# Attention's elementwise steps moved from GpSimd to VectorE and ScalarE, with longer scans and products

## The chip, the cores and the metric

The kernel runs on one core of a Trainium2 chip. Its time is the device time of one execution, in microseconds, as the median of the runs shown. The profile is of one execution on that core. PE is TensorE, DVE is VectorE, ACT is ScalarE, POOL is GpSimd and SP is the engine that issues most DMAs. [...]

## The reference, cut to what matters

An attention with complex decays, then two mixing stages. B=4 batches, H=8 heads, S=768 tokens, D=48.

```python
scale = np.minimum(mag, 0.999) / (mag + 1e-06)      # mag = |a_re + i a_im|
a_re_n, a_im_n = (a_re * scale, a_im * scale)
for t in range(S):
    new_re = ar * S_re - ai * S_im                  # ar, ai: a_re_n, a_im_n of token t
    new_im = ar * S_im + ai * S_re
    S_re, S_im = (new_re + k v^T, new_im)
    y[:, :, t] = q . S_re
...
h = x^T @ U @ V;  u = x + h^T                       # first stage, tokens mixed with rank 32
x = u + np.maximum(u @ w_ch1, 0.0) @ w_ch2          # width 384, hidden 1536
...
u = x + real(fft2(x));  un = layer norm of u        # second stage
out = u + np.maximum(un @ w_ch1, 0.0) @ w_ch2
```

## The kernel before, in words

The attention is worked in 24 chunks of 128 tokens (6 per batch), and its elementwise part in 12 pairs of chunks (PAIRS), 3 per batch. A tile of a pair is 128 partitions by 768 elements: 3 groups of channels, 2 chunks, 128 tokens.

`decays(m)` makes, for pair m, the running products of the decays and from them the scaled queries and keys. Its steps stand in order: squares of the parts of a (ACT), a range count (line 291, DVE), logarithm and exponential (line 87, ACT), `1 - 2e-6 s` (line 325, POOL, or DVE for the first batch), a product with a minimum (line 326, DVE), the tangent (line 337, POOL), a running product as three scans of 256 elements (line 340, DVE), a Newton step of the inverse root (lines 349, 353 and 354, two on POOL and one on DVE), and the two products with q and k (lines 359 and 360). `turns(m)` turns these tangents into angles (line 87, ACT), sums them along the tokens as three more scans (line 381, DVE), reduces them to one turn (lines 389 and 390), takes sine and cosine (ACT) and multiplies: per chunk four products of 384 elements (lines 408 and 409), three on DVE and one on POOL. The result QK goes through six DMAs per chunk into QT (line 412, SP).

`products(m, j)` does the matrix products of one chunk: scores (line 437), their mask (line 442, DVE), transposes of the keys (line 451), outputs y and state g (line 469). From the fifth chunk of batch 1 on the products are made of float16 parts: a cast on ACT (lines 445, 460, 486, 500, 567) and the remainder (lines 446 and 568 on POOL; 461, 487 and 501 on DVE). The keys are scaled once more in place (line 494, POOL).

The first mixing stage runs over b, g (halves of 384 tokens) and f (12 slices of the hidden width). For each f, `mm3` (lines 91 to 93) makes hp = w1 u from (hi, lo) pairs in three products; ACT makes hh = relu(hp) (line 182), DVE its remainder hl (line 184), and a step later lines 91 to 93 add w2 hh, w2 hh and w2 hl into acc. The attention of batch b+1 runs beside the first stage of batch b: `Side` hands out its steps. `make_ut` transposes x (line 617), copies it to SBUF (line 622, ACT), adds the low-rank token part from another PSUM bank (lines 626 and 627) and splits the sum into a pair u (lines 629 and 630). `from_f64` and `load_w` (lines 108 to 142) make float32 pairs of the float64 weights. The DFT and the second mixing stage follow.

The framework's scheduler sets the order on each engine from a simulated timeline and from priorities that the code gives (hh and hl are high), and each engine runs its instructions strictly in that order.

Of the kernel before, what the change touches and what calls it, by code (L numbers as in the profile page):

```python
# [13 lines left out]
I16 = mybir.dt.int16  # L14
AF = mybir.ActivationFunctionType
# [6 lines left out]
DM = H * D  # L22
# [19 lines left out]
def mixer_kernel(ctx, tc, a_in, qk_in, v_in, u_in, v4_in, w_in, cc_in, ss_in, cb_in, sb_in, id_in, mask_in, rows_in, out):  # L42
# [69 lines left out]
    def from_f64(src, name, signs=False):  # L112
# [22 lines left out]
    def load_w(mi, f, z):  # L135
# [4 lines left out]
        x = from_f64(w_in[mi, f][:, zs], f"w{mi}_{f}_{z}", mi == 1 or f > 8)  # L140
# [50 lines left out]
    # ------------------------------------------------------------------ attention  # L191
# [40 lines left out]
    def load_vs():  # L232
        """All values of the first batch."""
# [18 lines left out]

    def parts(m):
        """The first pair goes chunk by chunk, so that its products start early."""
        return [slice(0, 1), slice(1, 2)] if m == 0 else [slice(0, 2)]

    def decays(m):
        """Decayed queries and keys of a pair of chunks and the tangents of its turns."""
# [3 lines left out]
        E = G if b else V  # L262

# [3 lines left out]
        if b == 0:  # L267
            T_, s1, s2 = a[:, 1], mk("L"), mk("s")
            qf, kf = qk[:, 0], qk[:, 1]
        else:  # L270
            T_, s1, s2 = mk("T"), mk("L"), mk("s")
            qf, kf = s1, s2
        Th = a[:, 0] if b == 0 else mk("Th")
# [3 lines left out]
        ew[m] = T_, Th, qf, kf, ends  # L277
# [26 lines left out]
        for js in jj:  # L304
            re, im, s1_, s2_ = of(js, a[:, 0], a[:, 1], s1, s2)
            if at_once:
# [5 lines left out]
                steady(js)  # L312
# [22 lines left out]
        for js in jj:  # L335
# [3 lines left out]
            for i in range(3):  # L339
                V.tensor_tensor_scan(out=row(s1, i, js), data0=starts[:, :n], data1=row(s1, i, js), initial=1.0, op0=ALU.max, op1=ALU.mult)  # L340
# [3 lines left out]
        for js in jj:  # L344
            s1_, s2_, th = of(js, s1, s2, Th)
            tabled(s2_, s1_, AF.Ln)
            tabled(s2_, s2_, AF.Exp, bias=lnhalf, scale=-0.5, accum_out=stat("decay", b, cc[js.start]))
            A.activation(th, s2_, AF.Square, scale=2.0)
            (G if m == 2 or b else V).tensor_tensor(th, s1_, th, ALU.mult)
        yield  # L350
        for js in jj:
            s1_, s2_, th = of(js, s1, s2, Th)
            V.scalar_tensor_tensor(out=s2_, in0=th, scalar=3.0, in1=s2_, op0=ALU.subtract, op1=ALU.mult, reverse0=True)
            (G if m in (1, 2) or b else V).tensor_tensor(s1_, s1_, s2_, ALU.mult)
            V.tensor_copy(ends[:, :, js], s1_[:, :, :, 127])
# [869 lines left out]
```

## Time and profile before

| | |
|---|---|
| median of 3 runs | 1040.34 us (1038.24 to 1041.38) |
| span of the profiled execution, first to last instruction | 1035.1 us |
| its own time | not recorded beside the span; the median lies 5.2 us above the span |
| busy: PE, DVE, ACT, POOL | 885.1, 690.3, 441.3, 443.3 us |
| mean granted TensorE clock | 0.949 |

The span has five parts. Until 78 us the first batch's elementwise work runs and PE is mostly idle. Until 130 us the first batch's products run. From 130 to 518 us the first mixing stage runs with the attention of the later batches beside it. From 518 to 725 us that stage ends, and the weights of the second are made. From 725 us the second stage runs alone.

A busy engine is not always working: the duration of an instruction in the trace holds the time for which it could not go on.

### The profile page before, as it was taken

The page shows a single profiled execution, that of the slowest core. Times are in us where ns is not written, and L with a number is a line of the kernel's source. Part 1 is how long each engine was busy: PE and PEld are TensorE (multiplying, and loading weights), DVE is VectorE, ACT ScalarE, POOL GpSimd, SP SyncE. Part 2 cuts the span into 40 slices and gives each one's busy share as a digit, 9 for nine tenths or more (in the row PEclk, how much of TensorE's full clock was granted, in tenths as well). Part 3 has the DMA queues.
Part 4 walks back from the last instruction along what each step waited for, and adds up shares of the span by engine and source line. Part 5 has one row for each costly group of instructions (what it writes and reads, how often), then busy time and mean ns, then how long its engine had stood idle before and what let it go on. Part 6 is the DMA issues. An engine that isn't in the chain of part 4 may idle for free. (4 is left out here: it accounts for less than half of the span.)

```text
span 1035.1 us, 16471 instructions
## 1 busy us (share of the span) xinstructions
PE 885.1 (86%) x6338; PEld 841.7 (81%) x6338; DVE 690.3 (67%) x1104; ACT 441.3 (43%) x841; POOL 443.3 (43%) x426
## 2 busy tenths in 40 slices
PE   0059978788778787798899999779999999999997
PEld 0048777578777787787899999779999999999997
DVE  7997988897877689788764727886535554362121
ACT  6436565657545555555643224465212211222111
POOL 4445646575464645656446307776312222020000
PEclk9999899979898898989899999889999999999999
DMA  8078646834516152614135103342101021000000
GB/s 346 0 103 165 194 81 138 166 69 109 94 45 121 49 93 69 115 48 93 33 61 200 39 1 115 108 144 77 62 16 47 2 77 46 1 23 19 7 23 27
DMA packets 47097, 83.43 MB, mean 81 GB/s; under 512 B 5600, under 2 KB 36064, under 8 KB 47008
## 3 DMA queue, kind: packets, MB, share of 16 engines
q1 hardware_dynamic: 45152, 75.96, 30.8%
q0 software_dynamic: 1856, 6.31, 1.7%
q8 instruction: 52, 0.85, 0.4%
q14 instruction: 37, 0.30, 0.1%
HBM read 53.79 MB, written 9.44 MB: 61 GB/s over the span
## 5 line engine op out<-in xcount | busy, mean ns | idle before, releaser
L184 DVE SCALAR_TENSOR_TENSOR hl<-hp,hh 128x384 fp32r<-128x384 f32 x192 | 105.4, 551 | 191.8 <-ACT hh L182 186.6
L182 ACT ACTIVATE hh<-hp 128x384 fp32r<-128x384 f32 x192 | 93.1, 488 | 270.9 <-PE hp L93 249.1
L91 PE MATMUL acc<-w,hh 128*128 128x384 f32 x576 | 202.4, 352 | 2.0 <-ACT hh L182 2.0
L93 PE MATMUL acc<-w,hl 128*128 128x384 f32 x576 | 166.1, 352 | 38.4 <-DVE hl L184 38.2
L92 PE MATMUL acc<-w,hh 128*128 128x384 f32 x576 | 197.4, 343 | 0.0
L93 PEld LDWEIGHTS acc<-w,hl 128*128 128x128 f32 x576 | 106.9, 195 | 45.4 <-DVE hl L184 45.1
L91 PEld LDWEIGHTS acc<-w,hh 128*128 128x128 f32 x576 | 111.4, 193 | 4.3 <-ACT hh L182 3.0
L92 PEld LDWEIGHTS acc<-w,hh 128*128 128x128 f32 x576 | 111.5, 194 | 0.0
L91 PE MATMUL hp<-u,w 128*128 128x384 f32 x288 | 103.0, 359 | 6.2 <-ACT w L141 3.1
L92 PE MATMUL hp<-u,w 128*128 128x384 f32 x288 | 103.7, 360 | 1.2 <-POOL u L630 1.0
L93 PE MATMUL hp<-u,w 128*128 128x384 f32 x288 | 102.4, 356 | 0.0
L92 PE MATMUL hp<-n,w 128*128 128x384 f32 x288 | 96.9, 336 | 1.6 <-DVE n L920 1.6
L91 PE MATMUL hp<-n,w 128*128 128x384 f32 x288 | 96.5, 336 | 1.1 <-ACT n L919 1.1
L93 PE MATMUL hp<-n,w 128*128 128x384 f32 x288 | 96.8, 336 | 0.0
L437 PE MATMUL sc<-QT 96*128 96x128 f32 x384 | 66.6, 328 | 11.4 <-DMA QT<-QK 10.5
L437 PEld LDWEIGHTS sc<-QT 96*128 96x128 f32 x384 | 60.7, 232 | 14.3 <-issue 11.3
L142 POOL TENSOR_TENSOR w<-wxw,w 128x384 fp32r<-128x384 f32 x48 | 58.8, 1235 | 21.9 <-ACT w L141 21.7
L451 PE MATMUL kp<-ident,QK 128*128 128x128 f32 x120 | 20.5, 297 | 53.7 <-POOL QK L409 48.6
L91 PEld LDWEIGHTS hp<-u,w 128*128 128x128 f32 x288 | 58.5, 203 | 7.0 <-ACT w L141 3.3
L451 PEld LDWEIGHTS kp<-ident,QK 128*128 128x128 f32 x120 | 16.1, 155 | 55.5 <-POOL QK L409 48.6
L92 PEld LDWEIGHTS hp<-u,w 128*128 128x128 f32 x288 | 58.6, 203 | 2.2 <-POOL u L630 1.6
L93 PEld LDWEIGHTS hp<-u,w 128*128 128x128 f32 x288 | 58.3, 203 | 0.0
(302 smaller groups left out, 2056.4 us busy)
## 6 DMA issues: line engine op xcount, KB each, us to landing
QT<-QK SPq DMA_DIRECT2D x144, 129.0 KB
stw<-in_w_dram SPq DMA_DIRECT2D x48, 384.0 KB
ain<-in_a_dram SPq DMA_DIRECT2D x12, 768.0 KB
qkin<-in_qk_dram SPq DMA_DIRECT2D x12, 768.0 KB
x1d<-x SPq DMA_DIRECT2D x24, 192.0 KB
vin<-in_v_dram SPq DMA_DIRECT2D x18, 192.0 KB
lo<-x1d SPq DMA_DIRECT2D x12, 192.0 KB
out_dram<-lo SPq DMA_DIRECT2D x12, 192.0 KB
```

The lines of the kernel that those rows point to most:

```text
L91: T.matmul(o, ah, bh, start=start, stop=False, skip_group_check=skip)
L92: T.matmul(o, ah, bl, start=False, stop=False, skip_group_check=skip)
L93: T.matmul(o, al, bh, start=False, stop=stop, skip_group_check=skip)
L142: G.tensor_tensor(w[:, 1, zs], x, f32(w[:, 0, zs]), ALU.subtract)
L182: A.activation(hh, hp, AF.Relu)
L184: V.scalar_tensor_tensor(out=hl, in0=hp, scalar=0.0, in1=f32(hh), op0=ALU.max, op1=ALU.subtract)
L437: T.matmul(ps[:, h, :], q[:, 128:256], q[:, :128], start=True, stop=True)
L451: T.transpose(kp[z][:, i * 128 : (i + 1) * 128], QK[:, z, i, 128:256], ident)
```

## The change

- Moved from POOL to DVE: lines 349, 354, 446, 556, 568 and 630, part of 359 and 551, and the sign of the weights (line 128, which becomes the DVE form of line 130 everywhere).
- Moved from POOL or DVE to ACT: lines 325, 389 (later batches) and 494. The count of line 291 becomes two Relu passes with a sum on ACT for the later batches.
- Merged: three scans of 256 elements become one of 768, with a reset in a uint8 tile; the four products of a chunk's turn become two of 768, all on DVE, with sine and cosine in one tile `turn` of one buffer.
- `make_ut`: the low-rank product is added into the bank of the transposes, so that the copy of line 622 and the sum of line 627 go for all but the first group; u is split from PSUM.
- Buffers: tag t from 6 to 4, `turn` 1 of twice the size, vl from 2 to 1.

```diff
-            (V if z else G).tensor_tensor(QK[:, z, :, 128:256], kf[:, :, j], w[:, :, j], ALU.mult)
+                w = turn[:, :, :, j]
+                for to, x in ((slice(128, 256), kf), (slice(0, 128), qf)):
+                    V.tensor_tensor(QK[:, :, :, to], x[:, :, j].unsqueeze(1).to_broadcast([128, 2, 3, 128]), w, ALU.mult)
...
-            for i in range(3):
-                V.tensor_tensor_scan(out=row(s1, i, js), data0=starts[:, :n], data1=row(s1, i, js), initial=1.0, op0=ALU.max, op1=ALU.mult)
+            V.tensor_tensor_scan(out=flat(s1), data0=starts, data1=flat(s1), initial=1.0, op0=ALU.max, op1=ALU.mult)
...
+                if cy is not None:
+                    V.tensor_tensor(T_[:, :, 0, 0], T_[:, :, 0, 0], cy[:, :3], ALU.add)
+                V.tensor_tensor_scan(out=flat(Th), data0=going, data1=flat(T_), initial=0.0, op0=ALU.mult, op1=ALU.add)
...
-            (G if m == 2 or b else V).tensor_tensor(th, s1_, th, ALU.mult)
+            V.scalar_tensor_tensor(out=th, in0=s1_, scalar=FSCALE**2, in1=th, op0=ALU.mult, op1=ALU.mult)
...
-            E.tensor_scalar(s2_, s2_, -2e-6, 1.0, ALU.mult, ALU.add)
+            A.activation(s2_, s2_, AF.Copy, bias=1.0, scale=-2e-6)
...
+                    A.activation(Th[:, :, js], re, AF.Relu, bias=least, scale=-1.0, accum_out=stat("im", b, cc[0]))
+                    A.activation(Th[:, :, js], s2_, AF.Relu, bias=most, accum_out=stat("im", b, cc[1]))
...
-                for z in range(2):
-                    G.tensor_tensor(QK[:, z, :, 128:256], QK[:, z, :, 128:256], QK[:, z, :, 256:257].to_broadcast([128, 3, 128]), ALU.mult)
+                for i in range(3):
+                    A.activation(QK[:, :, i, 128:256], QK[:, :, i, 128:256], AF.Copy, scale=QK[:, 0, i, 256:257])
...
-                G.tensor_tensor(plo[:, hs], pm[hf], ph[:, hs], ALU.subtract)
+                V.tensor_tensor(plo[:, hs], pm[hf], ph[:, hs], ALU.subtract)
...
-            G.tensor_tensor(slo, sS, shi, ALU.subtract)
+            V.tensor_tensor(slo, sS, shi, ALU.subtract)
...
+            zv = bank(f"zv{b}_{g}_{k}")[:, :384] if first else xs[k]
+            T.matmul(zv, zst[b][:, k * 128 : (k + 1) * 128], vst[:, g * 384 : (g + 1) * 384], start=first, stop=True, skip_group_check=not first)
```

The first place is VectorE in the first mixing stage, batch 1, at the turn of pair (2, chunks 2 and 3): QK is the turned result, hl the remainder that PE waits for, kl and vl remainders of float16 parts, pm the masked scores. Before:

```order
L408 TENSOR_TENSOR QK2_2_2909<-L2_2_2630,Th2_2_2632 128x3x128
L487 SCALAR_TENSOR_TENSOR vl2_2_3102<-vin2_2_2932,vh2_2_3101 128x384
L184 SCALAR_TENSOR_TENSOR hl0_1_0_2_2806<-hp0_1_0_2_2734,hh0_1_0_2_2804 128x384
L442 TENSOR_TENSOR pm2_1_1_2895<-sc2_1_1_2863,mask_82 128x512
L461 SCALAR_TENSOR_TENSOR kl2_1_2900<-kp2_1_0_2903,kh2_1_2899 128x8x48
L405 COPY QK2_3_2934<-fe2_2_2634 128x6x2
L408 TENSOR_TENSOR QK2_3_2934<-L2_2_2630,T2_2_2629 128x3x128
L409 TENSOR_TENSOR QK2_3_2934<-s2_2_2631,T2_2_2629 128x3x128
L408 TENSOR_TENSOR QK2_3_2934<-L2_2_2630,Th2_2_2632 128x3x128
L461 SCALAR_TENSOR_TENSOR kl2_1_2900<-kp2_1_1_2926,kh2_1_2899 128x8x48
L184 SCALAR_TENSOR_TENSOR hl0_1_0_3_2861<-hp0_1_0_3_2824,hh0_1_0_3_2859 128x384
```

Now:

```order
L181 SCALAR_TENSOR_TENSOR hl0_1_0_3_2787<-hp0_1_0_3_2750,hh0_1_0_3_2785 128x384
L419 COPY QK2_3_2858<-fe2_2_2561 128x6x2
L423 TENSOR_TENSOR QK2_2_2835<-s2_2_2559,turn2_2_2557 128x6x128
L423 TENSOR_TENSOR QK2_2_2835<-L2_2_2558,turn2_2_2557 128x6x128
L423 TENSOR_TENSOR QK2_3_2858<-s2_2_2559,turn2_2_2557 128x6x128
L423 TENSOR_TENSOR QK2_3_2858<-L2_2_2558,turn2_2_2557 128x6x128
L476 SCALAR_TENSOR_TENSOR kl2_1_2826<-kp2_1_0_2829,kh2_1_2825 128x8x48
L476 SCALAR_TENSOR_TENSOR kl2_1_2826<-kp2_1_1_2850,kh2_1_2825 128x8x48
L181 SCALAR_TENSOR_TENSOR hl0_1_0_4_2848<-hp0_1_0_4_2811,hh0_1_0_4_2846 128x384
```

The pair's products now stand together, four of 768 elements between two hl, and the keys' share that was POOL's is among them.

The second place is the scaling of the keys of chunk (2, 2). On POOL before, with the small scaling fe ahead of it:

```order
L409 TENSOR_TENSOR QK2_2_2909<-s2_2_2631,Th2_2_2632 128x3x128
L556 TENSOR_TENSOR S2_1_3016<-S2_0_2773,fe2_1_2845 96x384
L494 TENSOR_TENSOR QK2_2_2909<-QK2_2_2909 128x3x128
L446 TENSOR_TENSOR ph2_1_2844<-pm2_1_0_2868,ph2_1_2844 128x512
L568 TENSOR_TENSOR Sl2_0_2810<-S2_0_2773,Sh2_0_2809 96x384
```

Now on ACT, where hh is made too:

```order
L319 ACTIVATE turn2_4_3033,stats_80<-ain2_4_2630,least_86 128x768
L320 ACTIVATE turn2_4_3033,stats_80<-s2_4_3035,most_87 128x768
L509 ACTIVATE QK2_2_2835<-QK2_2_2835 128x2x128
L88 ACTIVATE s2_4_3035<-L2_4_3034 128x768
L179 ACTIVATE hh0_1_0_5_2966<-hp0_1_0_5_2927 128x384
L509 ACTIVATE QK2_2_2835<-QK2_2_2835 128x2x128
L501 ACTIVATE vh2_3_3248<-vin2_3_3109 128x384
L509 ACTIVATE QK2_2_2835<-QK2_2_2835 128x2x128
```

The scaling is three instructions instead of two; it can run only when the DMAs have read QK, and hh stands behind it. The first of the two Relu passes waits for the last product of the pair before, which reads `turn`.

The third place is VectorE at the start, where the first chunk's angles are summed (ain is the first batch's tile). Before:

```order
L349 TENSOR_TENSOR ain0_2_107<-L0_2_142,ain0_2_107 128x768
L353 SCALAR_TENSOR_TENSOR s0_2_143<-ain0_2_107,s0_2_143 128x768
L110 TENSOR_SCALAR stu_260<-stu_260 128x192
L110 TENSOR_SCALAR stv0_269<-stv0_269 128x384
L381 SCALAR_TENSOR_TENSOR ain0_0_105<-one_83,ain0_0_105 128x128 x3
```

Now:

```order
L356 SCALAR_TENSOR_TENSOR ain0_2_114<-L0_2_149,ain0_2_114 128x768
L111 TENSOR_SCALAR stv0_265<-stv0_265 128x384
L360 SCALAR_TENSOR_TENSOR s0_2_150<-ain0_2_114,s0_2_150 128x768
L111 TENSOR_SCALAR stv1_274<-stv1_274 128x384
L361 SCALAR_TENSOR_TENSOR L0_2_149<-L0_2_149,s0_2_150 128x768
L392 SCALAR_TENSOR_TENSOR ain0_0_112<-one_83,ain0_0_112 128x128 x3
```

The product of line 354 (now 361) for the second pair stands ahead of the scans; it was POOL's.

## Rows read from the trace of the kernel before

**Rows 1.** Stretches: start:end and length, busy (instructions) by engine, PEclk, DMA share, GB/s.
```profile
0.00:78.00 78.00, 16.20 (x97) 13.50 (x98) 70.51 (x96) 37.89 (x62) 33.97 (x30) 1.00 0.55 150
...
130.00:518.00 388.00, 319.96 (x2516) 298.67 (x2517) 315.73 (x412) 224.21 (x404) 218.14 (x187) 0.89 0.43 88
518.00:621.00 103.00, 101.19 (x782) 99.29 (x781) 52.17 (x91) 34.84 (x75) 39.55 (x46) 1.00 0.26 75
621.00:725.00 104.00, 93.14 (x534) 89.23 (x533) 82.90 (x154) 52.58 (x111) 73.86 (x78) 0.93 0.36 111
```
**Rows 2.** Groups of PE, 130 to 518 us: busy, mean ns, idle before and its releasers.
```profile
L93 PE MATMUL acc<-w,hl 128*128 128x384 f32 x171 | 54.3, 380 | 31.5 <-DVE hl L184 31.4
...
L469 PE MATMUL g<-vh,kh 128*128 128x48 f16 x72 | 4.7, 187 | 13.3 <-DVE kl L461 13.3
```
**Rows 3.** DVE in order of time, 260 to 267 us: start, us, instruction.
```profile
262.93 2.95 DVE L487 SCALAR_TENSOR_TENSOR vl<-vin,vh 128x384 f16<-128x384 f32 x1
...
266.40 0.52 DVE L184 SCALAR_TENSOR_TENSOR hl<-hp,hh 128x384 fp32r<-128x384 f32 x1
```
**Rows 4.** POOL in order of time, the same stretch.
```profile
261.83 1.87 POOL L568 TENSOR_TENSOR Sl<-S,Sh 96x384 f16<-96x384 f32 x1
263.67 1.79 POOL L360 TENSOR_TENSOR s<-qkin,s 128x768 f32<-128x768 f32 x1
```
**Rows 5.** PE in order of time, the same stretch.
```profile
266.98 1.33 PE L93 MATMUL acc<-w,hl 128*128 128x384 f32 x3 [6.42 <-DVE hl L184]
```
**Rows 6.** DVE in order of time, two places where POOL did not read beside it.
```profile
136.04 1.85 DVE L381 TENSOR_TENSOR_SCAN Th<-one,T 128x256 f32<-128x256 f32 x3 [1.06 <-ACT T L87]
...
257.16 0.94 DVE L353 SCALAR_TENSOR_TENSOR s<-Th,s 128x768 f32<-128x768 f32 x1
```
**Rows 7.** Groups of DVE, 130 to 518 us.
```profile
L381 DVE TENSOR_TENSOR_SCAN Th<-one,cy,T 128x256 f32<-128x256 f32 x18 | 29.5, 1683 | 0.0
L340 DVE TENSOR_TENSOR_SCAN L<-starts,L 128x256 f32<-128x256 bf16 x24 | 28.7, 1249 | 0.1
...
L326 DVE SCALAR_TENSOR_TENSOR L<-L,s 128x768 f32<-128x768 f32 x8 | 21.0, 2621 | 16.8 <-POOL s L325 16.8
L408 DVE TENSOR_TENSOR QK<-L,T 128x384 f32<-128x384 f32 x17 | 15.2, 900 | 0.3 <-ACT T L87 0.3
...
L409 DVE TENSOR_TENSOR QK<-s,T 128x384 f32<-128x384 f32 x17 | 11.8, 700 | 0.0
...
L381 DVE TENSOR_TENSOR_SCAN Th<-one,T 128x256 f32<-128x256 f32 x9 | 8.8, 1026 | 1.1 <-ACT T L87 1.1
...
L627 DVE TENSOR_TENSOR xs<-zv,xs 128x384 f32<-128x384 f32 x16 | 8.6, 549 | 1.9 <-PE zv L626 1.9
...
L389 DVE TENSOR_SCALAR T<-Th 128x768 f32<-128x768 f32 x9 | 7.2, 801 | 0.0
```
**Rows 8.** Groups of POOL, 130 to 518 us: costliest, a middle and the smallest that goes.
```profile
L446 POOL TENSOR_TENSOR ph<-pm,ph 128x512 f16<-128x512 f32 x23 | 30.6, 1334 | 16.9 <-ACT ph L445 16.9
...
L494 POOL TENSOR_TENSOR QK<-QK 128x384 f32<-128x384 f32 x21 | 19.1, 910 | 17.4 <-DMA QT<-QK 10.1 <-DVE hl L184 3.9 <-DVE kl L461 3.4
...
L526 POOL TENSOR_TENSOR Sl<-S,Sh 96x384 f16<-96x384 f32 x1 | 1.3, 1297 | 0.0
```
**Rows 9.** DVE, then POOL, in order of time at the start.
```profile
36.00 5.79 DVE L381 TENSOR_TENSOR_SCAN ain<-one,ain 128x128 f32<-128x128 f32 x3
...
35.79 1.97 POOL L354 TENSOR_TENSOR L<-L,s 128x768 f32<-128x768 f32 x1 [3.04 <-DVE s L353]
```
**Rows 10.** ACT in order of time, 270 to 272 us.
```profile
270.90 0.49 ACT L182 ACTIVATE hh<-hp 128x384 fp32r<-128x384 f32 x1 [2.71 <-PE hp L93]
271.28 0.84 ACT L87 ACTIVATE T<-Th 128x768 f32<-128x768 f32 x1
```
**Rows 11.** Waits of POOL, 130 to 518 us: total, times, longest.
```profile
POOL fe L491 <- DMA QT<-QK: 19.3, 9, 6.1
...
POOL QK L494 <- DMA QT<-QK: 10.1, 6, 2.5
```

More of the change, by code (lines that the diff above doesn't have):

```diff
@@ L110, in kept, with from_f64 @@
             fn(*args, **kw)
-    def from_f64(src, name, signs=False):
+    def from_f64(src, name):
         n = src.shape[-1]
@@ L276, in decays @@
         jj = [slice(0, 2)]
-        ew[m] = T_, Th, qf, kf, ends
+        ew[m] = T_, Th, qf, kf, ends, a if b == 0 else turn
         def of(js, *xs):
@@ L368, in turns @@
         at = attention_pool()
-        T_, Th, qf, kf, ends = ew[m]
+        T_, Th, qf, kf, ends, turn = ew[m]
         use(TRIG)
@@ L612, in make_ut @@
         xs = {}
+        first = (b, g) == (0, 0)
         def turn(k):
-            xp = bank(f"xp{b}_{g}_{k}")[:, :384]
+            xs[k] = bank(f"xp{b}_{g}_{k}")[:, :384]
             for t in range(3):
-                T.transpose(xp[:, t * 128 : (t + 1) * 128], xt[b, g * 3 + t][:, k * 128 : (k + 1) * 128], ident)
-            if (b, g) == (0, 0):
+                T.matmul(
+                    xs[k][:, t * 128 : (t + 1) * 128],
+                    xt[b, g * 3 + t][:, k * 128 : (k + 1) * 128],
+                    ident,
+                    is_transpose=True,
+                    start=t == 0,
+                    stop=first and t == 2,
+                    skip_group_check=True,
+                )
+            if first:
+                xp = xs[k]
                 xs[k] = xpl[0].tile([128, DM], F32, tag="x", name=f"xs0_0_{k}", bufs=10)
-            else:
-                xs[k] = slot(f"xs{b}_{g}_{k}")
-            A.copy(xs[k], xp)
+                A.copy(xs[k], xp)
         def mix(k):
-            zv = bank(f"zv{b}_{g}_{k}")[:, :384]
-            T.matmul(zv, zst[b][:, k * 128 : (k + 1) * 128], vst[:, g * 384 : (g + 1) * 384], start=True, stop=True)
-            V.tensor_tensor(xs[k], zv, xs[k], ALU.add)
+            zv = bank(f"zv{b}_{g}_{k}")[:, :384] if first else xs[k]
+            T.matmul(
+                zv,
+                zst[b][:, k * 128 : (k + 1) * 128],
+                vst[:, g * 384 : (g + 1) * 384],
+                start=first,
+                stop=True,
+                skip_group_check=not first,
+            )
+            if first:
+                V.tensor_tensor(xs[k], zv, xs[k], ALU.add)
             u = pair(f"u{b}_{g}_{k}")
             A.copy(u[:, 0], xs[k])
-            (V if (b, g) == (0, 0) else G).tensor_tensor(u[:, 1], xs[k], f32(u[:, 0]), ALU.subtract)
+            V.tensor_tensor(u[:, 1], xs[k], f32(u[:, 0]), ALU.subtract)
             pieces.append(u)
@@ L641, in make_ut @@
             return
-        turn(0)
-        yield
-        turn(1)
-        mix(0)
-        yield
-        turn(2)
-        yield
-        mix(1)
-        yield
-        mix(2)
-        yield
+        for k in range(3):
+            turn(k)
+            mix(k)
+            yield
+            if k < 2:
+                yield
     def extra1(b, g, t, acc):
@@ L933, in mixer_kernel @@
     lnhalf = const("lnhalf", [128, 1])
-    starts = const("starts", [128, 2, 128], BF16)
     halfpi = const("halfpi", [128, 1])
+    least = const("least", [128, 1])
+    most = const("most", [128, 1])
     ust = const("ust", [128, NC, 4, 32], F32R)
@@ L941, in mixer_kernel @@
     G.memset(lnhalf, math.log(0.5))
-    G.memset(starts, 0.0)
-    G.memset(starts[:, :, 0:1], FSCALE**2)
-    starts = starts.rearrange("p x t -> p (x t)")
     G.memset(halfpi, PI / 2)
+    G.memset(least, RE_LEAST)
+    G.memset(most, -((IM_MOST / 2) ** 2))
     apool, dpool = ExitStack(), ctx.enter_context(ExitStack())
@@ L949, in mixer_kernel @@
     attp = [apool.enter_context(tc.tile_pool(name="att", bufs=2)), None]
+    starts = attp[0].tile([128, 6, 128], U8, tag="starts", name="starts", bufs=1)
+    going = attp[0].tile([128, 3, 256], U8, tag="going", name="going", bufs=1)
+    for x, every, rest_ in ((starts, 1, 0), (going, 0, 1)):
+        G.memset(x, rest_)
+        G.memset(x[:, :, 0:1], every)
+    starts = starts.rearrange("p x t -> p (x t)")
+    going = going.rearrange("p i t -> p (i t)")
     first = ExitStack()
@@ L966, in mixer_kernel @@
             with tc.issue_after(after):
-                T.matmul(warm, starts[:, :128], starts, start=True, stop=True, skip_group_check=True)
+                T.matmul(warm, mask, wide.bitcast(F16), start=True, stop=True, skip_group_check=True)
     first.close()
```

79 lines of the change are left out of this document (44 added, 35 removed).

## The prediction

> **What bounds the kernel now.** I read the table of stretches first, to find where TensorE does not work. In the first mixing stage, 130 to 518 us, PE is busy 320.0 of 388 us, so 68 us are idle, and the mean granted clock is 0.89 [rows 1]. From 518 to 621 us PE is busy 101.2 of 103, from 621 to 725 us 93.1 of 104. After 725 us (not in a row) PE works nearly throughout, and nothing that the change touches runs there. So what there is to win lies in the 388 us, with a little behind and ahead of them.
>
> The groups of PE by releaser come next: 31.4 us of the idle time stand ahead of `acc<-w,hl` and were ended by the remainder hl of DVE, 13.3 ahead of `g<-vh,kh` and were ended by kl of DVE [rows 2]. Together that is 44.7 of 68. Yet DVE is busy 315.7 of 388 us [rows 1]; it isn't full, but it is late, and the question is why.
>
> The third view shows it, DVE and POOL in order of time. At 262.93 DVE starts a remainder of 128x384 that lasts 2.95 us [rows 3]; a sum of 128x384 takes 0.55 in the mean (549 ns) [rows 7], and hl, of that size too, 0.52 [rows 3]. Over the same time POOL runs L568 (to 263.70) and L360 (to 265.46) [rows 4], and the DVE instruction ends at 265.88, after POOL does. hl runs only at 266.40, and PE, idle for 6.42 us, goes on at 266.98 [rows 5]. So DVE instructions that read two SBUF operands are stretched while POOL reads SBUF. Quiet prices are in rows 6: three scans of 256 elements 1.85 us, a two-operand pass over 768 elements 0.94. In the stage the scans take 1.68 and 1.25 us each instead of 0.62, and L326, a pass over 768, takes 2.62 instead of 0.94 [rows 7]. This is what moving work off POOL could cure.
>
> **The change on DVE, 130 to 518 us.** What goes, from rows 7: the scans of L381, 29.5 + 8.8, and of L340, 28.7; the turn's three groups of 17 products (15.2 the first, 11.8 the last), 40.5; L627, 8.6; L389, 7.2; eight counts of L291, taken at 0.94, 7.5. Sum 130.8. What comes, at quiet prices: 17 merged scans at 1.85 (the elements are the same), 31.5; 34 turn products of 768 at 0.94, 32.0; 17 passes over 768 from L349, L354 and L359, 16.0; 23 plo of 512 elements at 0.68, between 0.55 and 0.94, 15.6; 39 small passes (Sl, u, sh, the sign) at 0.55, 21.5. Sum 116.6. Then the stretching. Over quiet prices, L381 with the carry costs 29.5 - 18 x 0.62 = 18.3, L340 13.9, the turn's products 40.5 - 51 x 0.55 = 12.4 and L326 21.0 - 8 x 0.94 = 13.5, in all 58.1. POOL loses 13 groups, from L446 with 30.6 to L526 with 1.3 [rows 8], 162.1 of 218.1 us; it keeps 56, a quarter, and I let the stretching fall to a quarter, 15. DVE: 315.7 - 130.8 + 116.6 - 13.5 + 15 = **303 us**. The bounds are 288 (none left) and 333 (all 44.6 of the other three groups stay, should POOL's rest meet the same instructions). DVE's work thus hardly falls; what changes is that long stretched instructions ahead of hl become short ones.
>
> **What that gives PE.** I take half of the 44.7 us of waits, -22. The bounds are 0 and -44.7. Half, because a late hl comes in two kinds: one instruction stretched, as at 262.93, which goes, and several in a row ahead of hl, which stays: the four turn products of a pair now stand together, 4 x 0.94 = 3.8 us. The clock follows. At 0.89 in the mean, with two levels, 0.22 of the stretch is at the lower one; PE's work in it loses half its time, 0.11 x 320 = 35 us at most. The waits on hl and kl are 0.66 of the idle time, so 23 us hang on them, and half of these is **-12**; bounds 0 and -35.
>
> **ACT.** It gains 16 Relu passes, 8 of L325 and 9 of L389 at 0.84 (an Activate over 768 elements) and 32 key scalings at no more than 0.49 (over 384) [rows 10], and loses some 14 copies of L622 of that size: 224 + 27.7 + 15.7 - 6.9 = 261 of about 354 us. hh of 0.49 us stands between these and waits at most 0.84 more each time, which the step between hh and its use covers. I cost it at nothing; if that cover is gone, it is the slower rival below.
>
> [...]
>
> **The ends.** At the start three scans of 128 take 5.79 us beside a 1.97 us product of POOL, L354 [rows 9], where twice the elements take 1.85 quiet [rows 6]: at most -3.9. L349 and L354 of the second pair go to DVE instead, 2 x 0.94 = +1.9, on an engine that is busy 70.5 of 78 us [rows 1]. Between these I take -1. From 621 to 725 us, 10.9 us are idle and POOL is busy 73.9 [rows 1]; the signs of the weights leave it. Bounds 0 and -10.9; I take half, -5.
>
> **Edits at nothing.** The low-rank part in PSUM drops a copy on ACT and a sum on DVE (counted above); PE's products are as many as before. vl with one buffer waits for g of the chunk before, whose end Sl next to it needs as well: at most 0.55 each, hidden by the steps to its use. `turn` with one buffer makes the Relu of the next pair wait for the last turn product, at most 3.8 us, 8 times, on ACT, far ahead of that pair's use; cover gone, 30 us on ACT, of which it has 90 free. QK's DMAs are as many, but leave SP only when both products are done: at most 0.94 later per chunk, in a chain that starts a pair ahead. vh, ph and the other casts are as before.
>
> **The sum.** -22 - 12 - 1 - 5 = -40. The profiled span is 1035.1; 995 and the 5.2 us by which the median lies above the span give **1000 us**.
>
> **Rivals.** *PE is set free wholly.* All waits on hl and kl and their clock go: -44.7 - 23 - 6 = -74, 966 us. For it: the stall at 262.93 is of the kind that goes wholly. Against: DVE would have 303 of 320 us to work, without room. 0.20.
>
> *DVE stays late.* Its share of the stage rises from 0.81 to 303/354 = 0.86, and scans of 1.85 and four products in a row can't be interrupted by hl. Then a quarter goes, -11 - 6 = -17: 1023 us. 0.20.
>
> *It doesn't do what it says.* POOL keeps L360 and the tangent beside the scans, the stretching moves to the merged ones (333 us on DVE), and PE waits as before: 1040 us. 0.05.
>
> *Slower: ACT is held by the keys.* The scaling of L494 must wait until DMAs have read QK. On POOL that wait delays only POOL: 10.1 us in 6 waits on L494, 19.3 in 9 on L491 just ahead, the longest 6.1 [rows 11, 8]. On ACT hh stands behind it in strict order, and without hh neither hl nor acc. 21 instructions of two per chunk are 11 chunks; 11 x 6.1 = 67 us if each waits as long as the longest, and 1000 + 67 = 1067. It decides from a mean wait of 40/11 = 3.6 us per chunk. Against it: the mean of the 15 waits is 2.0, and the order puts other work of ACT ahead of the scaling. 0.08.
>
> **How the numbers follow.** The forecast has 0.47, the rivals as above. The range reaches from below the free PE, 955, to above the late DVE, 1034; outside are the rival of no gain, the slower one and the tail of the free one, some 0.16. About 0.3%, or 3 us, is what a measurement of this kernel can tell from no change. Faster is 0.47 + 0.20 + 0.20 = 0.87, same 0.05, slower 0.08.
>
> **What would show it.** Right: the first mixing stage about 354 us long; idle time ahead of `acc<-w,hl` near 16 instead of 31 and ahead of g near 7; merged scans near 1.85, turn products near 0.94; DVE about 303 us there, POOL about 56, ACT about 260; PEclk above 0.92. Wrong: turn products or scans well over these prices; idle time of PE that hh of ACT ends, with ACT waiting for the DMAs of QT ahead of the scaling; a stage after 725 us that is longer; or a start that ends later than 78 us.

## The result and the profile after

The changed kernel takes 1027.28 us (median of 4, 1023.83 to 1030.17) against 1039.29 before: a ratio of 0.9882 with a 95% interval of 0.9856 to 0.9907. It is faster by 12 us where 40 were forecast. The profiled executions fell from a span of 1035.1 us to one of 1022.1.

To compare the same work, the span is cut here by work instead of by time: at the first product `hp<-u` (the first mixing stage begins), at the end of the last y or g (the attention ends), and at the end of PE's last product. Before these are at 133.0, 552.5 and 1028.5 us, after at 136.4, 546.6 and 1015.5. The start thus grew by 3.4, the middle shrank by 9.3 (419.5 to 410.2) and the end by 7.1 (476.0 to 468.9). The cut is not exact: the middle holds 2884 instructions of PE before and 2893 after.

The page of the kernel after, busy time of each engine:

```profile
PE 878.7 (86%) x6338; PEld 832.0 (81%) x6338; DVE 651.0 (64%) x1117; ACT 465.3 (46%) x880; POOL 232.2 (23%) x249
```

Stretches of the kernel before, then after, from the first mixing product to the attention's end; columns as in [rows 1]. The third number from the end is PEclk, the granted clock of TensorE as a share; slices of 0.25 us read 1.00 at most and 0.50 at least:

```profile
133.00:552.50 419.50, 352.95 (x2884) 331.13 (x2885) 335.03 (x442) 238.11 (x433) 232.19 (x201) 0.90 0.42 85
```

```profile
136.40:546.60 410.20, 353.79 (x2893) 330.43 (x2894) 300.59 (x452) 275.19 (x500) 70.11 (x66) 0.90 0.46 88
```

GpSimd fell by 162 us, as the steps said, and VectorE by 34, where the steps gave 13. But PE is busy as long as before at the same mean clock of 0.90, and its idle time only fell from 66.6 to 56.4 us.

VectorE's groups after, 130 to 518 us, those that answer to [rows 7]:

```profile
L423 DVE TENSOR_TENSOR QK<-L,turn 128x768 f32<-128x768 f32 x18 | 18.7, 1044 | 0.0
L389 DVE TENSOR_TENSOR_SCAN turn<-going,turn 128x768 f32<-128x768 uint8 x9 | 17.4, 1931 | 0.0
L423 DVE TENSOR_TENSOR QK<-s,turn 128x768 f32<-128x768 f32 x18 | 17.1, 954 | 2.8 <-ACT turn L88 2.8
L347 DVE TENSOR_TENSOR_SCAN L<-starts,L 128x768 f32<-128x768 uint8 x8 | 14.0, 1752 | 0.1
L334 DVE SCALAR_TENSOR_TENSOR L<-L,s 128x768 f32<-128x768 f32 x8 | 7.6, 954 | 1.7 <-ACT s L333 1.7
```

The quiet prices of [rows 6] hold: a merged scan takes 1.93 or 1.75 us, a turn product 0.95 to 1.04, and L334, which was L326 with 2.62, takes 0.95.

What PE waited for, kernel before, 133.0 to 552.5 us (engine, line, releaser: total, times, longest):

```profile
PE acc L93 <- DVE hl L184: 31.4, 12, 6.4
PE g L469 <- DVE kl L461: 15.1, 6, 5.4
...
PE hp L91 <- DVE hl L184: 2.2, 1, 2.2
...
PE acc L91 <- ACT hh L182: 1.6, 3, 0.9
```

The same of the kernel after, 136.4 to 546.6 us:

```profile
PE sc L452 <- DMA QT<-QK: 11.2, 4, 4.6
PE acc L92 <- ACT hh L179: 7.5, 8, 1.9
PE y L484 <- DVE ph L461: 6.8, 4, 4.1
PE xp L650 <- DVE zst L620: 6.3, 2, 5.7
PE sc L452 <- issue: 6.2, 2, 4.6
PE hp L92 <- ACT u L661: 5.4, 2, 2.8
PE g L484 <- DVE kl L476: 4.2, 2, 2.5
PE acc L94 <- DVE hl L181: 4.0, 3, 1.9
```

The waits on hl and kl fell from 48.7 (31.4 + 15.1 + 2.2) to 8.2. In their place stand waits that hardly existed: for the DMAs that turn QK into QT, for hh of ScalarE, for plo (named ph), for zst and u.

### The profile page after: what moved, and what is told of

It reads as the page before. It is cut to its first block, busy times and chain, and to the rows that moved or that the text cites. A ratio compares the mean times of both kernels' runs of the same rounds, so it can differ in the third digit from the quotient of the medians.

```text
span 1022.1 us, 16249 instructions
## 1 busy us (share of the span) xinstructions
PE 878.7 (86%) x6338; PEld 832.0 (81%) x6338; DVE 651.0 (64%) x1117; ACT 465.3 (46%) x880; POOL 232.2 (23%) x249
## 4 chain that ended last, share of the span: by engine, by line
PE 54%; DVE 20%; DMA 12%; SPq 4%; issue 4%; ACT 4%; POOL 2%; DVEq 0%; ACTq 0%; POOLq 0%
DMA QT<-QK 8%; PE acc L94 7%; PE acc L92 7%; PE hp L92 7%; PE hp L93 7%; PE hp L94 7%; PE acc L93 7%; PE sc L452 4%; SPq L427 4%; DMA stw<-in_w_dram 3%; PE g L484 2%; PE y L484 2%; DVE QK L423 1%; DVE ph L461 1%; DVE wxw L126 1%
## 5 line engine op out<-in xcount | busy, mean ns | idle before, releaser
L94 PE MATMUL acc<-w,hl 128*128 128x384 f32 x576 | 161.2, 349 | 11.9 <-DVE hl L181 11.8
L92 PEld LDWEIGHTS acc<-w,hh 128*128 128x128 f32 x576 | 109.8, 191 | 12.0 <-ACT hh L179 10.8
L93 PEld LDWEIGHTS acc<-w,hh 128*128 128x128 f32 x576 | 109.8, 191 | 0.0
L92 PE MATMUL hp<-u,w 128*128 128x384 f32 x288 | 101.1, 356 | 5.4 <-ACT u L661 5.4
L93 PE MATMUL hp<-u,w 128*128 128x384 f32 x288 | 102.1, 355 | 3.1 <-DVE u L662 3.1
L94 PE MATMUL hp<-u,w 128*128 128x384 f32 x288 | 101.1, 352 | 0.0
L92 PEld LDWEIGHTS hp<-u,w 128*128 128x128 f32 x288 | 57.0, 200 | 6.8 <-ACT u L661 6.7
L93 PEld LDWEIGHTS hp<-u,w 128*128 128x128 f32 x288 | 57.3, 199 | 4.8 <-DVE u L662 4.7
L94 PEld LDWEIGHTS hp<-u,w 128*128 128x128 f32 x288 | 57.3, 199 | 0.2
```

Of the source, the lines that this page charges most:

```text
L92: T.matmul(o, ah, bh, start=start, stop=False, skip_group_check=skip)
L93: T.matmul(o, ah, bl, start=False, stop=False, skip_group_check=skip)
L94: T.matmul(o, al, bh, start=False, stop=stop, skip_group_check=skip)
```

## The experiments

Times are medians, the ratio is to the kernel before in the same runs, with its 95% interval. The last columns come from the profile of one execution, with the cuts named above: the first `hp<-u`, the length from there to the attention's end, and PE's waits on hl and kl in that length. Executions of one kernel lie up to 15 us apart (e11, 1006.6 us at a granted clock of 0.961 to 1021.4 at 0.942), so a difference in these columns counts only where several kernels show it.

| kernel | us | ratio | first hp | length | hl + kl |
|---|---|---|---|---|---|
| before | 1039.3 | 1 | 133.0 | 419.5 | 48.7 |
| bn1: before, other order | 1034.2 | 0.9978 (0.9955 to 1.0000) | 132.8 | 409.3 | 29.3 |
| after | 1027.3 | 0.9882 (0.9856 to 0.9907) | 136.4 | 410.2 | 8.2 |
| n1: after, other order | 1018.5 | 0.9825 (0.9779 to 0.9872) | 132.1 | 406.2 | 11.5 |
| n2: after, other order | 1027.7 | 0.9901 (0.9872 to 0.9930) | 139.9 | 410.4 | 10.7 |
| e1: warm matmuls | 1028.7 | 0.9893 (0.9840 to 0.9945) | 142.4 | 407.6 | 6.4 |
| e3: keys on GpSimd | 1013.0 | 0.9778 (0.9735 to 0.9822) | 138.3 | 394.1 | 6.7 |
| e3, other order | 1017.6 | 0.9780 (0.9730 to 0.9830) | 142.7 | 395.6 | 5.7 |
| e4: products of 384 | 1013.4 | 0.9766 (0.9727 to 0.9805) | 128.4 | 411.4 | 8.1 |
| e2: and six buffers | 1003.4 | 0.9658 (0.9610 to 0.9707) | 131.9 | 397.3 | 9.2 |
| e2, other order | 1004.1 | 0.9678 (0.9646 to 0.9710) | 128.0 | 396.1 | 7.2 |
| e9: e2 and e3 | 995.5 | 0.9601 (0.9573 to 0.9630) | 128.0 | 385.3 | 5.9 |
| e9, other order | 1004.3 | 0.9678 (0.9646 to 0.9710) | 125.9 | 396.9 | 7.6 |
| e5: first batch off GpSimd | 1017.9 | 0.9782 (0.9741 to 0.9822) | 144.0 | 403.3 | 9.7 |
| e7: signs on GpSimd | 1018.1 | 0.9813 (0.9792 to 0.9833) | 135.3 | 399.1 | 5.5 |
| e8: QT on GpSimd's queue | 1044.8 | 1.0058 (1.0023 to 1.0094) | 151.6 | 418.1 | 9.5 |
| e10: short passes back | 1023.7 | 0.9832 (0.9758 to 0.9906) | 138.3 | 404.8 | 5.2 |
| e11: GpSimd loaded | 1014.4 | 0.9770 (0.9700 to 0.9839) | 135.9 | 395.3 | 12.6 |
| e12: e11, scans of 256 | 1014.0 | 0.9772 (0.9741 to 0.9804) | 135.6 | 400.5 | 17.2 |
| m2: before, moves alone | 1007.9 | 0.9704 (0.9669 to 0.9739) | 130.0 | 394.1 | 12.7 |

**How much an order alone does.** Any edit makes the scheduler write another order, so two runs changed only the pace of the side work, and one did so to the kernel before:

```diff
-                side = Side(attention(b + 1), (58, 48, 48)[b], 40)
+                side = Side(attention(b + 1), (59, 48, 48)[b], 40)
```

> The changed kernel with nothing moved but the pace at which the side work of batch 1 is handed out (59 steps per 40 slots instead of 58): the same instructions in another order. If the 14 and 24 us of the runs with the keys, the products or the buffers undone are due to these edits: within 5 us of 1027. If any other order does as much: 10 us or more away from 1027.

The second, with (58, 49, 48):

> The changed kernel with another pace of the side work alone (49 steps instead of 48 in batch 2). The first such run took 1018.5. If the changed kernel's order happens to be a poor one: 1014 to 1022. If it is ordinary and the first was lucky: 1025 to 1031.

The kernel before, with 59:

> The kernel before with the pace of the side work alone changed (59 steps instead of 58 in batch 1). If the order of the kernel before is an ordinary one: 1033 to 1044. If it is a well chosen one, as a tuned order would be: 1046 to 1060.

n1 took 1018.5, n2 1027.7, and the kernel before 1034.2. An order is worth up to 9 us in time, and up to 12 in the length of the middle (e9, 385.3 and 396.9). It also moves the waits: the kernel before waits 48.7 us for hl and kl, in its other order 29.3, and is only 4 us faster. So no single run within some 9 us of 1018 to 1028 says anything about its edit. What follows rests on edits that stand out of that, or that show the same in several kernels.

**The moves alone, in the kernel before.** This run (m2) makes most of the moves from GpSimd to VectorE and no other part of the change: scans, the turn's products, the moves to ScalarE, `make_ut`, the signs and the buffers stay as before.

```diff
-                G.tensor_tensor(plo[:, hs], pm[hf], ph[:, hs], ALU.subtract)
+                V.tensor_tensor(plo[:, hs], pm[hf], ph[:, hs], ALU.subtract)
...
-            G.tensor_tensor(slo, sS, shi, ALU.subtract)
+            V.tensor_tensor(slo, sS, shi, ALU.subtract)
```

> The kernel before with its GpSimd passes of lines 349, 354, 359, 446, 526, 551, 556 and 568 moved to VectorE as in the change, and nothing else: scans, turn products, buffers, key scaling and signs as before. GpSimd's busy time in the first mixing stage falls from 218 to about 115 us. If GpSimd beside VectorE makes hl and kl late: VectorE's excess over quiet prices falls from 105 to under 75 us, PE's waits on hl and kl from 49 to under 25, time 1015 to 1030. If VectorE's own load does: VectorE rises to over 350 us, the waits stay over 40, time 1036 to 1055.

It took 1007.9 us: 19 less than the whole change. Its stretch, and PE's waits in it, 130.0 to 524.0 us:

```profile
130.00:524.00 394.00, 343.18 (x2889) 320.56 (x2890) 332.96 (x514) 241.25 (x435) 137.66 (x134) 0.93 0.46 91
```

```profile
PE acc L93 <- DVE hl L184: 12.4, 10, 2.5
PE y L469 <- DVE pm L442: 8.9, 4, 3.7
PE zv L626 <- DVE zst L605: 5.7, 2, 4.3
```

VectorE is as busy as before the change (333 of a shorter 394 us), and yet the waits on hl and kl are 12.7 us. So its load alone did not make hl late; that GpSimd's work beside it did fits (137.7 us busy in this stretch, 232.2 before), but it is argued: m2 ran in one order, and an order alone took the waits from 48.7 to 29.3. The 30 us of time are far more than an order. PE's idle time fell by 15.7 us, less than half of what the waits on hl and kl fell by (36.0), since other waits came in their place here too. The clock came back, 0.93 for 0.90.

**The turn's products and their buffers.** Two runs gave these back, with the products all on VectorE. First the products alone (e4), which keeps the one buffer `turn`:

```diff
-                for to, x in ((slice(128, 256), kf), (slice(0, 128), qf)):
-                    V.tensor_tensor(QK[:, :, :, to], x[:, :, j].unsqueeze(1).to_broadcast([128, 2, 3, 128]), w, ALU.mult)
+                for z, w in ((1, T_), (0, Th)):
+                    V.tensor_tensor(QK[:, z, :, :128], qf[:, :, j], w[:, :, j], ALU.mult)
+                    V.tensor_tensor(QK[:, z, :, 128:256], kf[:, :, j], w[:, :, j], ALU.mult)
```

> The changed kernel with only the turn's products as four of 384 per chunk, the one buffer turn kept. If the burst of merged products makes QT late: QT waits of PE under 6 us and 1018 to 1023. If the single buffer does: waits as now (over 12 us) and 1027 to 1033, and the run with six buffers is faster than this one by over 5 us.

Then the buffers as well (e2):

```diff
-            T_, s1, s2 = turn[:, 1], mk("L"), mk("s")
+            T_, s1, s2 = mk("T"), mk("L"), mk("s")
...
-        def at(nm, tag=None, bufs=4, shape=(128, 3, 2, 128), dt=F32, pl=pl):
+        def at(nm, tag=None, bufs=6, shape=(128, 3, 2, 128), dt=F32, pl=pl):
```

> The changed kernel with the turn's products as four of 384 per chunk again (all on VectorE) and T and Th in six buffers of tag t as before, the same memory. In the changed kernel PE waits for QT's DMAs 17.5 us from 130 to 530 us (11.2 named so and 6.2 as issue; 0 before the change). Theory B, the one buffer of turn and the burst of products make QT late: these waits fall under 6 us and the time falls to 1015 to 1021, though VectorE has about 6 us more to do. Rival, QT is late because of the order or of SP's queue: the waits stay over 12 us and the time is 1027 to 1033.

And e2 in another order:

> Buffers and products of 384 as in the run of 1003.4, but in another order (59 steps in batch 1). The changed kernel in three orders took 1018.5, 1027.3 and 1027.7, a spread of 9. If the buffers and products are a cost of their own: at most 1010. If 1003.4 was the luck of an order: 1013 to 1025.

e4 took 1013.4, faster than both of its theories had it, and e2 1003.4 and 1004.1, faster than e4 by over 5 us, as that of the one buffer had it. Against the changed kernel in the same two orders (1027.3 and 1018.5) that is 24 and 14 us: this much of the change went here. The two parts seem to show in different places. With merged products the first mixing product comes at 132.1 to 144.0 us in eleven kernels, 138.3 in the mean; with products of 384 at 125.9 to 131.9 in five, 128.4 in the mean (e8 is left out). The merged ones thus cost about 10 us at the start. How is not settled. The twelve DMAs of a pair leave SP in one row after the four merged products, and this row is not what comes late. VectorE and SP's queue in the kernel after, at the third pair of batch 0:

```profile
86.49 3.55 DVE L423 TENSOR_TENSOR QK<-qkin,ain 128x768 f32<-128x768 f32 x4
```

```profile
88.37 11.46 SPq L427 DMA_DIRECT2D QT<-QK  x12
```

And SP's queue in e2:

```profile
83.42 3.79 SPq L421 DMA_DIRECT2D QT<-QK  x6
100.42 4.12 SPq L421 DMA_DIRECT2D QT<-QK  x6
```

The last product of the turn ends at 90.0 us after the change and at 84.6 in e2, but the last DMA of the batch has left SP at 99.8 us after the change and at 104.5 in e2; in the mean it is 100.3 in the eleven kernels and 100.7 in the five. The difference comes behind it: the last low-rank product `z<-x` ends at 129.8 and 123.0 us in the mean, and the first `hp<-u` follows 8.5 and 5.4 us later. In the kernel after, PE waits there for sums on VectorE:

```profile
132.22 1.33 PE L650 MATMUL zv<-vst,zst 128*128 128x384 f32 x3 [5.24 <-DVE zst L620]
```

The buffers show in the middle: with one buffer and products of 384 (e4) it lasts 411.4 us, with six buffers 397.3 and 396.1. In time that is 10 us; e4 ran in one order only. The stretches of e4 and of e2:

```profile
128.40:539.80 411.40, 351.54 (x2910) 327.09 (x2911) 302.34 (x484) 272.13 (x496) 62.62 (x63) 0.91 0.45 87
```

```profile
131.90:529.20 397.30, 342.58 (x2886) 321.92 (x2887) 304.30 (x484) 271.24 (x495) 67.86 (x64) 0.92 0.45 90
```

But the expected sign did not come: PE's waits for QT are 17.3 us in e2 (9.1 named so and 8.2 as issue), as many as in the kernel after, and 11.7 in its other order. Nor does one kind of time account for the gain: against the kernel after, e2's PE idles 1.7 us less and is busy 11.2 less, at a clock of 0.92 for 0.90; in its other order it idles 9.6 less and is busy 4.5 less. By which waits one buffer costs time is not settled.

**The keys on ScalarE.**

```diff
-                for i in range(3):
-                    A.activation(QK[:, :, i, 128:256], QK[:, :, i, 128:256], AF.Copy, scale=QK[:, 0, i, 256:257])
+                for z in range(2):
+                    G.tensor_tensor(QK[:, z, :, 128:256], QK[:, z, :, 128:256], QK[:, z, :, 256:257].to_broadcast([128, 3, 128]), ALU.mult)
```

> The changed kernel with the key scaling back on GpSimd. ScalarE waits 24.3 us (18 times) for DMAs at this scaling, and PE 7.5 us for hh. Theory C, hh is late behind the scaling: PE's waits on hh fall under 2 us and the time falls to 1020 to 1024. Rival, GpSimd's 19 us more stretch VectorE as before the change: VectorE's waits on hl and kl rise from 8 to over 14 us and the time is 1028 to 1035.

In another order:

> The key scaling on GpSimd, as in the run of 1013.0, in another order (59 steps). The plain changed kernel with 59 steps took 1018.5. If the scaling on ScalarE is a cost of its own: 1004 to 1014. If not: 1016 to 1028.

With the buffers and products undone as well, in two orders:

> The changed kernel with the products of 384, T and Th in six buffers (1003.4 us by itself) and the key scaling on GpSimd (1013.0 by itself) together. If both are separate costs that add up: 1003.4 - 14 = 989, from 985 to 994. If both only relieve the same chain of the attention: 1000 to 1006.

> Both undone, as in the run of 995.5, in another order. If they are costs of their own: 990 to 1002. If luck: over 1008.

The middle lasts 394.1 and 395.6 us with the keys on GpSimd, against 410.2 and 406.2 of the change in the same two orders. In the whole time it is 1013.0 against 1027.3 in the first order, but 1017.6 against 1018.5 in the second, where the first `hp<-u` comes 10.6 us later (142.7 for 132.1). The expectation for the second order, 1004 to 1014 for a cost of its own and 1016 to 1028 for none, thus came out against it. GpSimd's 16 to 18 us more did no harm: hl and kl wait 6.7 and 5.7. On top of the buffers and products the keys gave 8 us in one order (995.5) and none in the other (1004.3). So a cost of the keys' scaling on ScalarE is not shown. e9 is the fastest kernel of the study in its first order; its two times lie on either side of the forecast of 1000.

The way in which the scaling was to do harm is in the trace, but it is small. ScalarE after the change, in order of time at a chunk of batch 3, and the wait over 130 to 530 us:

```profile
430.59 0.92 ACT L320 ACTIVATE turn<-s,most 128x768 f32<-128x768 f32 x1
...
434.27 0.51 ACT L509 ACTIVATE QK<-QK 128x256 f32<-128x256 f32 x1 [2.65 <-DMA QT<-QK]
...
436.87 0.51 ACT L509 ACTIVATE QK<-QK 128x256 f32<-128x256 f32 x1 [0.56 <-DMA QT<-QK]
437.29 0.47 ACT L179 ACTIVATE hh<-hp 128x384 fp32r<-128x384 f32 x1
```

```profile
ACT QK L509 <- DMA QT<-QK: 24.3, 18, 3.4
```

hh stands behind the scaling that waits for DMAs, and PE behind hh: its product at 437.81 waited 1.94 us.

```profile
437.81 0.44 PE L92 MATMUL acc<-w,hh 128*128 128x384 f32 x1 [1.94 <-ACT hh L179]
```

Over 130 to 530 us PE waits 7.5 us for hh in all. With the scaling on GpSimd these waits were to fall under 2 us; in e3 they rose:

```profile
PE acc L92 <- ACT hh L179: 11.3, 7, 6.8
```

So if the middle is shorter in e3, it is not by hh.

**Does GpSimd's load bring the waits back?** e10 gave it plo, Sl and the state's scaling again, e11 also three passes of 768 elements per pair, e12 scans of 256 on top:

```diff
-            V.tensor_tensor(slo, sS, shi, ALU.subtract)
+            G.tensor_tensor(slo, sS, shi, ALU.subtract)
```

> The changed kernel with the remainders plo and Sl and the scaling sh of the state back on GpSimd (some 40 instructions, about 50 us there from 130 to 520 us, about 29 us off VectorE at their mean there). The forecast's reason, GpSimd beside VectorE makes hl and kl late: VectorE's excess over quiet prices rises from 31 to over 45 us, PE's waits on hl and kl from 8 to over 16, the time from 1027 (or 1018 in another order) to 1030 to 1040. Rival, VectorE is relieved and the chain of the attention decides: 1008 to 1018.

```diff
-            V.scalar_tensor_tensor(out=th, in0=s1_, scalar=FSCALE**2, in1=th, op0=ALU.mult, op1=ALU.mult)
+            (G if b else V).tensor_tensor(th, s1_, th, ALU.mult)
...
-            (G if m in (1, 2) else V).tensor_tensor(f, q, s1_, ALU.mult)
+            (G if m in (1, 2) or b else V).tensor_tensor(f, q, s1_, ALU.mult)
```

> The changed kernel with GpSimd loaded nearly as before: for the later batches the line 1 - 2e-6 s, the product of line 349 and the queries by their decays (8 passes of 768 elements each) and the remainders and the state's scaling of the earlier run on GpSimd; its busy time in the first mixing stage goes from 70 to about 170 us. The forecast's reason, GpSimd beside VectorE makes hl and kl late: VectorE's excess there goes from 32 to over 60 us, PE's waits on hl and kl from 8 to over 25 us, time 1030 to 1042. Rival, VectorE's load and order made them late, not GpSimd: waits on hl and kl under 12 us, time 1012 to 1026.

```diff
-            V.tensor_tensor_scan(out=flat(s1), data0=starts, data1=flat(s1), initial=1.0, op0=ALU.max, op1=ALU.mult)
+            for i in range(3):
+                V.tensor_tensor_scan(out=row(s1, i, js), data0=starts[:, :n], data1=row(s1, i, js), initial=1.0, op0=ALU.max, op1=ALU.mult)
```

> The run with GpSimd loaded (1014.4 us, waits on hl and kl 12.6 us, excess 54) with each merged scan as three scans of 256 elements again. If merging the scans is what spared hl and kl from GpSimd, since each scan by itself can be held: excess over 75 us, waits on hl and kl over 25, time 1025 to 1040. If it is the other edits (turn products, count and copies off VectorE): excess 50 to 65, waits under 18, time 1010 to 1022.

e10 took 1023.7 us, between its two theories, with waits on hl and kl of 5.2. The stretch of e11:

```profile
135.90:531.20 395.30, 341.70 (x2870) 317.29 (x2871) 284.06 (x390) 266.87 (x488) 169.99 (x132) 0.92 0.47 91
```

With 170 us on GpSimd, hl and kl wait 12.6 us and the kernel is no slower. So GpSimd's work alone does not bring these waits back, nor did VectorE's load alone in m2. One reading, not tested further, is that both are needed: with VectorE at 284 us it has the room to be held up, with 335 before the change it had not, and with 333 and GpSimd at 138 (m2) it wasn't held up enough. Where between 170 and 232 us of GpSimd the waits begin was not tried. The merged scans gave nothing in time (1014.0 without, 1014.4 with), though hl and kl wait 4.6 us less with them.

**Start, end and queue.** 36 more warm matmuls ahead of the first low-rank product (e1):

```diff
-    for after, n in zip(scored[:1] + ends, [20, 4, 0, 0, 0, 0, 4]):
+    for after, n in zip(scored[:1] + ends, [20, 40, 0, 0, 0, 0, 4]):
```

> The changed kernel with 40 instead of 4 warm matmuls in the last group, ahead of the first low-rank product. In the changed kernel PE idles 5.2 us there, the clock falls to the lower level and the first hl ends at 148.9 us (139.1 before the change, where 17 warm matmuls stood in this place). Theory A, the loss at the start is the clock after that gap: the first hl ends 4 to 6 us earlier and the time falls from 1027 to 1020 to 1023. Rival, the waits on u and hh behind the gap (2.8, 1.6, 0.9 and 1.9 us) take the clock down again: first hl within 2 us of 148.9 and time 1025 to 1030.

1028.7 us, and the first hl ended at 149.2 (148.9 in the kernel after): no gain. The first batch's two products off GpSimd (e5):

```diff
-            G.tensor_tensor(g, k, s2_, ALU.mult)
+            (V if b == 0 else G).tensor_tensor(g, k, s2_, ALU.mult)
```

> The changed kernel with the first batch's two products that stay on GpSimd (keys by their decays, state by its decay) on VectorE. In the changed kernel a copy of 6 elements on VectorE lasts from 122.9 to 127.5 us, as long as four GpSimd instructions run one after the other, and the low-rank sums behind it are 5 us late. If GpSimd's rest is what costs the start: the copy takes under 1.5 us, the first hl ends 4 to 6 us before 148.9, time 1019 to 1024. If VectorE's own load does: first hl not earlier, 1026 to 1032.

The long copy is gone (0.16 us), but the first hl ended at 154.2, later than without it; the 1017.9 us is within what an order does. The signs (e7):

```diff
+            A.activation(high.bitcast(F32), high.bitcast(F32), AF.Sign)
+            G.tensor_tensor(x, x, high.bitcast(F32), ALU.mult)
```

> The changed kernel with the signs of the later weights back on ScalarE and GpSimd (24 + 6 products there, as before). By the prediction, which gave the end -5 us: the stretch from the end of the attention to the last instruction, 468.9 us, grows by 3 to 7 us, time 1030 to 1034. By the traces, which show the end no shorter: within 2 us, time 1024 to 1029.

From the attention's end to PE's last product it takes 471.6 us against 468.9. But the other kernels with the signs on VectorE take 465 to 473 us there, so these 2.7 us show nothing of the signs; what shortened the end by 7.1 has not been traced. Half of QT's DMAs on GpSimd's queue (e8):

```diff
-                        nc.sync.dma_start(QT[p0 : p0 + 16], QK[:, z, i, :])
+                        (nc.gpsimd if z else nc.sync).dma_start(QT[p0 : p0 + 16], QK[:, z, i, :])
```

> The changed kernel with three of the six QT DMAs of a chunk issued by GpSimd's queue instead of SP's. The twelve of a pair now leave SP one after the other, about 0.65 us each. If the queue makes QT late: PE's waits on QT fall from 17.5 to under 10 us, time 1005 to 1015. If the transfer or the software queue's own latency does: 1016 to 1032.

1044.8 us, slower than before the change and outside both theories: GpSimd, which issues the DMAs, idles 56.0 us ahead of them until VectorE has made QK (11.36 of it at 446.45), and the tangents and the state's scaling stand behind them in its order; the first `hp<-u` comes at 151.6. So this run could not tell whether SP's queue is the limit.

## Why the prediction fell short

**VectorE: right in kind, and freer than forecast.** 303 us were forecast for 130 to 518 us and 290 measured, next to the bound of 288 at which no stretching is left; GpSimd 56 and 74, ScalarE 261 and 268. For the same work VectorE fell by 34 us, where the sum has 13. That an instruction of VectorE takes longer beside GpSimd is in the rows, with 2.95 us for a remainder whose size takes 0.55 [rows 3, 4, 7], and in the whole trace of the kernel before: `wxw<-wxw,stw` of 128x384 (L125) takes 0.51 to 0.57 us in 19 cases without GpSimd and up to 2.19 beside it; `stw<-stw` (L108), which reads one operand, takes 0.33 to 0.36 without and up to 2.16 beside it; hl, which has an operand in PSUM, takes at most 0.56 in all 192 cases. That this made hl and kl late is borne out by m2, but not shown alone (see there).

**The waits on hl and kl: sized too small.** I took -22 of 44.7; they fell by 40.5 of 48.7. The four products in a row, for which I kept half, hardly made hl late. That the order alone can take 19 us of them (bn1) was not known.

**The stage: the step that failed is "edits at nothing".** The forecast of the middle was -34 (-22 and the clock's -12), and the measured -9.3. The waits on hl and kl gave 40.5, but others took their place, so that PE's idle time fell by 10.1 only, and the clock, which I let follow the waits, stayed at 0.90. Its two levels are in the trace: of 4080 slices of 0.25 us of the kernel before 3650 read 1.00 and 388 read 0.50, and the products of hp follow each other every 0.32 us at 0.50 (from 134.31 us) and every 0.17 at 1.00 (from 137.30). How the clock hangs on the idle time the runs do not show: with 10.1 us less of it the clock stayed, in m2 it is 0.93 with 15.7 less. I had named the edits one by one and priced each at nothing, with a cover: the one buffer `turn` "far ahead of that pair's use", the products' DMAs "in a chain that starts a pair ahead", the keys' scaling "which the step between hh and its use covers". The runs show that the products and the one buffer are not free: undone together, in two orders, they give 24 and 14 us. Taken apart, the merged products cost about 10 us at the start (eleven kernels against five), and the one buffer 14 in the middle by one order of e4. For the keys no cost is shown.

With all three undone (e9) the change does what was forecast: 995.5 and 1004.3 us in two orders against 1000, and in the middle -34.2 and -22.7 against -34. m2, which has none of them, gives -25.5 in the middle, of it -15.7 of idle time and -9.8 of PE's busy time at a clock of 0.93 for 0.90. That the totals meet so closely is in part luck, since the waits on hl and kl fell by nearly twice the forecast and others came in their place.

What stays open is how. The largest new wait, PE's for QT, is 17.4 us in the kernel after and still 14.4 and 18.0 in e9, but 3.2 in m2 and 6.6 in e11, which has one buffer and merged products but three passes of each pair back on GpSimd. Which of the moved passes makes QT late was not tried by itself. Nor did a run undo `make_ut`, the Relu passes or the one buffer of vl.

**ScalarE held by the keys: the wait came, its harm is not shown.** It was given 0.08 as a rival. ScalarE waits 24.3 us for 33 instructions of three per chunk, so 2.2 us per chunk, below the 3.6 that I had as the point from which the whole change is slower. But PE's waits on hh did not fall when the scaling went back to GpSimd.

**The rival of a late VectorE came nearest, 1023, for a wrong reason.** hl and kl were not late.

**Readings.** The 0.80 us of L389 [rows 7] is a mean that passes of up to 2.03 us have raised; its median is 0.55 us, so a pass is cheaper on VectorE than the 0.84 that the sum gives it on ScalarE. The 303 us do not rest on this. The 5.2 us by which the median lay above the span were mostly spread between executions: every later one lies 1.7 to 2.2 us above its own span.

**Start and end.** -1 was forecast for the start and +3.4 measured; with products of 384 (e4) the first `hp<-u` comes at 128.4, which is -4.6. -5 was forecast for the end and -7.1 measured, for a reason that is not traced.

**The order.** That an order alone moves the time by up to 9 us was in no term. It is nearly a third of what the moves did by themselves, and of the three orders of the change its own is one of the two slower ones.

## What to carry to other kernels

When one wait is cured, others come in its place: an edit that is priced at nothing because something covers it must be priced again with that cover gone, above all a buffer less and merged work where work was spread. Take a change apart and run its main part alone in the old kernel: here the moves by themselves were worth 30 us and the rest gave 19 back. Where a scheduler writes the order, run a kernel in a second order before a few microseconds are put down to an edit. And let a run test the way in which an edit is said to do harm, not only its time: the waits that an edit was to cure (hh in e3, QT in e2) stayed.

## What the runs showed of the hardware

One instruction of VectorE lasted over several of GpSimd. VectorE, then GpSimd, in order of time, kernel after:

```profile
122.90 4.59 DVE L362 COPY fe<-L 128x6 f32<-128x6 f32 x1
...
460.92 0.16 DVE L362 COPY fe<-L 128x6 f32<-128x6 f32 x1
```

```profile
122.73 0.94 POOL L566 TENSOR_TENSOR S<-S,fe 96x384 f32<-96x384 f32 x1
123.63 0.99 POOL L139 TENSOR_TENSOR w<-wxw,w 128x384 fp32r<-128x384 f32 x1
124.59 1.81 POOL L367 TENSOR_TENSOR s<-qkin,s 128x768 f32<-128x768 f32 x1
126.35 0.99 POOL L139 TENSOR_TENSOR w<-wxw,w 128x384 fp32r<-128x384 f32 x1
```

A copy of 6 elements, which took 0.16 us at 460.92, took 4.59 here: it ended at 127.49, when the last of four GpSimd instructions that followed each other without a gap had ended (127.34; two memsets of 0.12 us each then ran to 127.46). I had reckoned with one instruction. Another copy did not last to the end of such a run. VectorE, then GpSimd, kernel before:

```profile
54.63 1.66 DVE L394 COPY cy<-ain 128x3 f32<-128x3 f32 x1
```

```profile
54.10 2.17 POOL L354 TENSOR_TENSOR L<-L,s 128x768 f32<-128x768 f32 x1 [5.50 <-DVE s L353]
56.23 1.80 POOL L360 TENSOR_TENSOR qkin<-qkin,s 128x768 f32<-128x768 f32 x1
```

This copy ended at 56.29, just after the first of two GpSimd instructions (56.27), though the second had begun at 56.23. The two copies ended 0.15 and 0.02 us after one of these GpSimd instructions, the remainder of [rows 3] 0.42 after L360 [rows 4]; what ends such a stretch, no run here tells.
